# Four attention tiles' exponentials taken set by set with their sums, and two rules of the planner

## The chip, the cores and the metric

The kernel runs on one core of a Trainium2 chip. The metric is the device time of one execution in microseconds, the median of the runs. The engines are called PE (TensorE, matmuls), ACT (ScalarE), DVE (VectorE), POOL (GpSimd) and SP (which issues most DMAs).

## The reference

Windowed attention (4 batches, 8 heads, 768 positions, head size 64), then a gated dense layer and a second dense layer with a rational activation, all in float32:

```python
scores = scale * np.matmul(q_c, k_full.transpose(0, 1, 3, 2))   # 32 queries, 64 keys (8 memory, 56 context)
scores = scores - np.max(scores, axis=-1, keepdims=True)
a = np.exp(scores)
a = a / (np.sum(a, axis=-1, keepdims=True) + 1e-09)
out[:, :, c_start:c_end] = np.matmul(a, v_full)
...
h = (1 / (1 + np.exp(-(x @ w_gate))) * (x @ w_val)) @ w_out     # 3072 x 512 tokens, 1536 features
h = h @ w_in                                                    # 2048 features
g = (a0 + a1*h + a2*h*h + a3*h*h*h) / (1 + abs(b0)*abs(h) + abs(b1)*h*h + 1e-6)
return g @ w_out2
```

## The kernel before

The 3072 tokens are 24 tiles of 128. Attention of a tile yields scores of 128 partitions by eight sets (`NSET`, one for each head) of 64 keys, in two PSUM places (`sp`, one for each half of the heads). Each matrix product of the dense layers is made of three products of rounded halves (`TERMS`), so a weight or an activation is split into a high part (ACT) and a rest (DVE), and weights come as 64-bit words that ACT (`conv_scale`, two activations) and DVE (`conv_bits`) first turn into float32.

Tiles 0 to 3 go first, one by one, in an opening that is written out at lines 1315 to 1384: loads, `attn_qk` (scores), `attn_max` (maximum and subtraction), `attn_exp`, `attn_sum` (sum and reciprocal), `attn_mul`, `attn_t` (four transposes, copied by ACT to `at`) and `pv` (`attn_pv`, product with the values into two places `xp`, split into `x` by ACT and DVE). Between them stand `idle_mm(n)`, n matmuls whose result nobody reads. Scores of a tile at the edge of a sequence (tiles 0 and 5, 6 and 11, ...) are copied to SBUF and masked by POOL; of the others, DVE reads the scores in PSUM. After the opening the loop over (token block, feature) begins with `gate_val` (`h`) for block 0, which needs `x` of tiles 0 to 3, and later tiles' attention is run between dense work: tiles 4 to 7 singly, from tile 8 in pairs, with functions `pair_*`.

The program isn't issued as written. `Recorder` records each call (`call`, line 240) with a duration from a formula (`cost`, line 205) as a task, finds what each depends on (`access`, line 269), and `plan` (line 314) simulates the engines and chooses each engine's order: PE's is the order written; on ACT, DVE, POOL and SP the ready task with the earliest due time (`t.late`) goes next. A due time is worked out backwards from those who need the result. A load of another activation table (exponential, sigmoid, reciprocal root) is charged 1.29 us in the plan. Tiles come from pools with a few places each: `ps` has four PSUM places, taken in turn, so the n-th tile of that pool waits for the users of the one four before it. Every user of a pool's tile other than its first one (`c.first`) depends on the first. What `plan` returns is issued by `emit` at line 471, so all instructions have that line in the profile.

Of the kernel before, what the change touches and what calls it, by code (L numbers as in the profile page):

```python
# [11 lines left out]
F32 = mybir.dt.float32  # L12
# [4 lines left out]
ACTF = mybir.ActivationFunctionType  # L17
ALU = mybir.AluOpType
AX = mybir.AxisListType
PSUM = bass.MemoryType.PSUM  # L20

B, H, S, D = 4, 8, 768, 64
CH, LEFT, RIGHT, NMEM = 32, 16, 8, 8
NT, DM, DFF1, DFF2 = B * S, H * D, 1536, 2048
P = 128
# [6 lines left out]
KEYS = NMEM + LEFT + CH + RIGHT  # L32
OFF1 = WIN - KEYS
NSET = 8
# [140 lines left out]
class Task:  # L175
    def __init__(self, eng):
        self.eng, self.calls, self.deps, self.cells, self.gets = eng, [], set(), set(), []
        self.dur, self.lat, self.bytes, self.start, self.table, self.mark = 0.0, 0.15, 0, None, None, None
        self.window, self.cap, self.soon, self.late, self.fixed = 30.0, None, 0.0, 0.0, False
        self.ordered = True  # L180
# [10 lines left out]
class Recorder:  # L191
# [48 lines left out]
    def call(self, eng, op, args, kw):  # L240
        out = kw.get("out", args[0] if args else None)
        reads = [x for x in (*args[0 if "out" in kw else 1 :], *kw.values()) if isinstance(x, Ref) and x is not out]
        reads = [x for x in reads if x is not kw.get("out")]
        key = {x.cell for x in reads}
        if eng == "tensor" and out.size() > 128:
            key.add(out.cell)
        same = eng == "tensor" and self.open is not None and self.open.key == key
        if same:
            t = self.open
        else:  # L250
            t = Task(eng)
            t.key, t.fixed, t.soon = key, self.fixed, self.ideal
            self.tasks.append(t)
            if eng == "tensor":
                self.open = t
                t.late = t.soon = self.ideal
            if self.noted is not None:
                self.noted.append(t)
        before = t.dur
        self.cost(t, op, args, kw)  # L260
        if eng == "tensor":
            self.ideal += t.dur - before
        t.calls.append((op, args, kw))
        for x, write in [(x, False) for x in reads] + ([(out, True)] if isinstance(out, Ref) else []):
            self.access(t, x, write)
        if eng != "tensor" and self.open in t.deps:
            self.open = None

    def access(self, t, x, write):
        c, box = x.cell, x.box()  # L270
        if c.pool is not None and t not in c.users:
            if c.first is None:
                c.first = t
                t.gets.append(c)
            elif c.first is not t:
                t.deps.add(c.first)
            c.users.add(t)
            t.cells.add(c)
        keep = []
        for b, u, w in c.accesses:  # L280
            if b[0] < box[1] and box[0] < b[1] and b[2] < box[3] and box[2] < b[3]:
                if u is not t and (write or w):
                    t.deps.add(u)
                inside = box[0] <= b[0] and b[1] <= box[1] and box[2] <= b[2] and b[3] <= box[3]
                if write and inside or u is t and w == write and inside:
                    continue
            keep.append((b, u, w))
        keep.append((box, t, write))
        c.accesses = keep
# [24 lines left out]
    def plan(self):  # L314
        tasks = self.tasks
        for t in tasks:
            t.succ = []
        for t in tasks:
            t.missing, t.soft = len(t.deps), []
            for d in t.deps:  # L320
                d.succ.append(t)
            t.ready = 0.0
# [6 lines left out]
        for t in reversed(tasks):  # L329
            t.succ, t.hard = t.succ + t.soft, t.succ  # L330
            if t.eng == "tensor":
                t.late = min([t.soon] + [u.late - t.lat * (u.eng != "tensor") - t.dur for u in t.succ])
                continue
            lat = t.lat + (4.5 if t.bytes else 0)
            cap = t.cap if t.cap is not None else self.DMA_CAP if t.bytes else self.CAP
            t.late = min([t.soon + cap] + [u.late - lat - t.dur for u in t.succ])
        free = dict(self.sizes)
        cells = {c for t in tasks for c in t.cells}
        for c in cells:
# [14 lines left out]
        ready = {e: [t for t in tasks if t.eng == e and not t.missing] for e in engines}  # L354
        busy, dma, table = dict.fromkeys(engines, 0.0), 0.0, None
        order, ends, half, now, stall, left = [], [], None, 0.0, 0.0, len(tasks)
        events = []
        self.stalls = []
        while left:
# [3 lines left out]
            for e in engines:  # L363
# [3 lines left out]
                if e == "tensor":  # L367
                    pick = pe[pe_i : pe_i + 1]
                elif head:
                    pick = head[:1]  # L370
                else:
                    pick = ready[e]
                best = None
                for t in pick:
                    if t.missing or t.ready > now + 1e-9 or best and best.late <= t.late:
                        continue
                    if not t.fixed and e != "tensor":
                        if t.late > now - stall + t.window:
                            continue
                        if t.bytes and dma > now + 7 and t.late > now - stall + 9:  # L380
                            continue
                    need, h = {}, half
                    for c in t.gets:
                        if c.pool == ("t", "half"):
                            if h:
                                h = None
                                continue
                            h = True
                        need[c.pool] = need.get(c.pool, 0) + 1
                    if all(  # L390
                        free[self.real_pool(p)] >= n + 2 * (n == 3) + (0 if t.fixed or p[0] not in (self.ORDERED if t.ordered else "g") else bisect_left(waiting[p], t.key))
                        for p, n in need.items()
                    ):
                        best = t
                if best is None:
                    continue
                t = best
# [10 lines left out]
                if t.table and t.table != table:  # L408
                    table, extra = t.table, 1.29
# [17 lines left out]
                for c in t.cells:  # L427
                    c.left -= 1
                    g = c.group
                    g[2] = max(g[2], end)  # L430
                    if c.left == 0:
                        g[1] += 1
                        if g[1] == 2 or g[1] == g[0] and g is not half:
                            heapq.heappush(ends, (g[2], self.real_pool(c.pool)))
                for u in t.hard:
                    u.missing -= 1
                    u.ready = max(u.ready, end if u.eng != e or e != "tensor" else now + t.dur)
                    if not u.missing and u.eng != "tensor":
                        ready[u.eng].append(u)
                    heapq.heappush(events, u.ready)  # L440
# [4 lines left out]
            if not moved:  # L445
# [5 lines left out]
                for e in engines[1:]:  # L451
                    for t in ready[e]:
                        w = t.late + stall - t.window
# [5 lines left out]
                now = max(nxt, now + 1e-6)  # L459
# [15 lines left out]
def fused_kernel(ctx: ExitStack, tc: tile.TileContext, q, k, v, w1, w2, coef, x2d, w2o, wq2, wqa, wqs, out):  # L475


    nc = Recorder(tc.nc)
# [10 lines left out]
    spool = pool("s", 4)  # L489
# [28 lines left out]
    qs, ks, vs, s_sb, sc_ps, at_sb = {}, {}, {}, {}, {}, {}  # L518
# [22 lines left out]
    def attn_qk(t):  # L541
# [28 lines left out]
        else:  # L570
            sc_ps[t] = sps

    def attn_max(t):
        s = s_sb[t]
        m = spool.tile([P, NSET, 1], F32, tag="m", name=f"m{t}")
        if edge(t):
            nc.vector.tensor_reduce(out=m[:, :, 0], in_=s, axis=AX.X, op=ALU.max)
            nc.vector.tensor_tensor(out=s, in0=s, in1=m.to_broadcast([P, NSET, KEYS]), op=ALU.subtract)
            return
        sv = s.rearrange("p (r h) w -> p r h w", h=2)  # L580
        mv = m.rearrange("p (r h) w -> p r h w", h=2)
        sps = sc_ps.pop(t)
        for h in range(2):
            nc.vector.tensor_reduce(out=mv[:, :, h, 0], in_=sps[h], axis=AX.X, op=ALU.max)
        for h in range(2):
            nc.vector.tensor_tensor(
                out=sv[:, :, h], in0=sps[h], in1=mv[:, :, h].to_broadcast([P, 4, KEYS]), op=ALU.subtract
            )

    def attn_exp(t):  # L590
        s = s_sb[t]
        nc.scalar.activation(out=s, in_=s, func=ACTF.Exp, scale=1.0 / float(D) ** 0.5)

    rs = {}

    def attn_sum(t):
        s = s_sb[t]
        r = rs[t] = spool.tile([P, NSET, 1], F32, tag="r", name=f"r{t}")
        nc.vector.tensor_reduce(out=r[:, :, 0], in_=s, axis=AX.X, op=ALU.add)
        nc.vector.tensor_scalar_add(out=r, in0=r, scalar1=1e-9)  # L600
        nc.vector.reciprocal(out=r, in_=r)

# [1463 lines left out]
```

## Time and profile before

| | |
|---|---|
| median of 3 runs | 1134.45 us (1133.39 to 1134.48) |
| the profiled execution | 1134.46 us |
| its span, first to last instruction | 1132.6 us |
| PE, ACT, DVE busy | 99%, 66%, 77% of the span |
| first `h` matmul starts | 29.86 us |
| activation table loads | 31, of 1.28 us each |

The views used are the busy times of the engines; the same by stretch of time, with the granted clock of TensorE (1.00 is 2.4 GHz, 0.50 is 1.2 GHz); the list of waits; the instructions of one engine in order of time, like ones merged; and the instructions grouped by shape. `out<-in` names the tiles; a tile's name can be that of another one that shares its place.

### The profile page before, as it was taken

What the parts mean: (1) busy time and instruction counts of PE and PEld (TensorE: products, weight loads), DVE (VectorE), ACT (ScalarE), POOL (GpSimd) and SP (SyncE); (2) the same over time, 40 slices, a digit from 0 to 9 for tenths busy, and PEclk for the clock granted to TensorE, in tenths of its full rate; (3) what the DMA queues carried; (4) which work ended last, traced back from release to release, by engine and by line L of the source; (5) the groups of instructions that cost most, each with busy time, mean ns of one, the idle gap of its engine ahead of it and who ended that gap; (6) DMA issues with size and microseconds to landing.
All of it is one profiled execution on the core that took longest, in us unless ns stands there. A gap on an engine that the chain in (4) does not pass through costs nothing.

```text
span 1132.6 us, 20033 instructions
## 1 busy us (share of the span) xinstructions
PE 1120.2 (99%) x7815; PEld 918.5 (81%) x7815; DVE 872.8 (77%) x1184; ACT 750.1 (66%) x1105; POOL 23.1 (2%) x39
## 2 busy tenths in 40 slices
PE   8999999999999999999999999999999999999998
PEld 4787888888888888888888788888888888888887
DVE  5788867774676667565568499999899999789984
ACT  4999556663454466343345599875799974898852
POOL 0000000000000000000000000000000000000000
PEclk8999999999999999999999999999999999999999
DMA  9899699997978799898976576689677788576764
GB/s 371 311 352 360 227 347 363 350 365 259 379 279 324 288 376 387 310 373 291 322 259 246 191 230 220 208 246 342 203 229 225 223 288 307 167 242 219 230 207 143
DMA packets 100318, 318.78 MB, mean 281 GB/s; under 512 B 10752, under 2 KB 11008, under 8 KB 100224
## 3 DMA queue, kind: packets, MB, share of 16 engines
q1 hardware_dynamic: 96192, 303.51, 74.3%
q0 software_dynamic: 3456, 12.58, 6.0%
q8 instruction: 62, 1.02, 0.4%
q10 hardware_dynamic: 576, 1.41, 0.3%
q14 instruction: 32, 0.26, 0.1%
HBM read 240.91 MB, written 63.96 MB: 269 GB/s over the span
## 4 chain that ended last, share of the span: by engine, by line
PE 96%; ACT 1%; DMA 1%; DVE 1%; issue 0%; DVEq 0%
PE acc L471 40%; PE p L471 20%; PE q_X L471 12%; PE h L471 10%; PE q_Z L471 6%; PE q_Y L471 3%; PE xp L471 2%; PE sp L471 1%; PE tp L471 1%; PE idle L471 1%; DMA st<-w_in 0%; DMA k<-k_in 0%; ACT L471 0%; ACT stp L471 0%; DVE s L471 0%
## 5 line engine op out<-in xcount | busy, mean ns | idle before, releaser
L471 PE MATMUL acc<-w2o,G 128*128 128x512 f32 x1152 | 268.4, 389 | 0.0
L471 PEld LDWEIGHTS acc<-w2o,G 128*128 128x128 f32 x1152 | 216.2, 188 | 44.9
L471 PE MATMUL acc<-g,wp 128*128 128x512 f32 x720 | 177.0, 393 | 0.0
L471 PEld LDWEIGHTS acc<-g,wp 128*128 128x128 f32 x720 | 133.3, 188 | 28.3 <-issue 0.2
L471 PE MATMUL q_X<-x,wi 128*128 128x512 f32 x576 | 146.5, 390 | 1.4 <-ACT hb L471 1.4
L471 PE MATMUL h<-x,wp 128*128 128x512 f32 x576 | 138.1, 392 | 1.7 <-ACT sg L471 0.9
L471 PE MATMUL p<-b,wpq_s 128*128 128x512 f32 x576 | 138.4, 389 | 0.0
L471 PEld LDWEIGHTS q_X<-x,wi 128*128 128x128 f32 x576 | 107.9, 188 | 24.7 <-ACT hb L471 2.5
L471 PEld LDWEIGHTS h<-x,wp 128*128 128x128 f32 x576 | 107.2, 188 | 25.0 <-ACT wp L471 1.1
L471 PEld LDWEIGHTS p<-b,wpq_s 128*128 128x128 f32 x576 | 108.1, 188 | 22.5
L471 ACT ACTIVATE st<-st 128x512 f32<-128x512 f32 (+1 forms) x124 | 76.7, 666 | 0.0
L471 PE MATMUL p<-x,wpq_a 128*128 128x512 f32 x288 | 73.2, 389 | 0.0
L471 PE MATMUL q_Z<-x,wi 128*128 128x512 f32 x288 | 73.1, 389 | 0.0
L471 ACT ACTIVATE u<-q,qc 128x1024 f32<-128x1024 f32 x48 | 54.9, 1147 | 14.4 <-DMA q<-u 13.2
L471 PEld LDWEIGHTS p<-x,wpq_a 128*128 128x128 f32 x288 | 54.0, 188 | 11.3
L471 PEld LDWEIGHTS q_Z<-x,wi 128*128 128x128 f32 x288 | 54.1, 188 | 11.2
L471 DVE SCALAR_TENSOR_TENSOR t<-t,cf,u 128x1024 f32<-128x1024 f32 x48 | 61.2, 1278 | 0.0
L471 DVE SCALAR_TENSOR_TENSOR q<-q,u 128x1024 f32<-128x1024 f32 x48 | 58.3, 1219 | 2.2 <-ACT u L471 2.1
L471 ACT ACTIVATE hb<-q_X 128x512 f32<-128x512 f32 x48 | 28.4, 592 | 36.4 <-PE q_X L471 36.3
L471 ACT ACTIVATE u<-u 128x1024 f32<-128x1024 f32 x48 | 50.3, 1055 | 0.4
L471 ACT ACT_TABLE_LOAD x31 | 39.8, 1283 | 15.8 <-PE h L471 7.2
L471 ACT ACTIVATE g<-c 128x512 fp32r<-128x512 f32 x22 | 13.8, 629 | 51.1 <-DVE c L471 51.1
(271 smaller groups left out, 1708.8 us busy)
## 6 DMA issues: line engine op xcount, KB each, us to landing
w2o<-w2o SPq DMA_DIRECT2D x96, 512.0 KB, 4.4
wi<-wq SPq DMA_DIRECT2D x72, 512.0 KB, 4.6
st<-w_in SPq DMA_DIRECT2D x62, 512.0 KB, 7.0
wp<-wqa SPq DMA_DIRECT2D x55, 512.0 KB, 6.6
wpq_s<-wqs SPq DMA_DIRECT2D x48, 512.0 KB, 8.1
wpq_a<-wqa SPq DMA_DIRECT2D x36, 512.0 KB, 7.6
wqa<-wp SPq DMA_DIRECT2D x30, 512.0 KB, 7.5
v<-v_in SPq DMA_DIRECT2D x24, 512.0 KB, 6.4
```

What stands on the lines that cost most here:

```text
L471: getattr(getattr(self.nc, t.eng), op)(*[real(x) for x in args], **{n: real(x) for n, x in kw.items()})
```

## The change

For tiles 0 to 3, `attn_max` no longer subtracts the maximum: it makes `nm`, the negative of the scaled maximum. `attn_exp` then runs one activation for each of the eight sets, of 64 keys, which reads the scores (of tile 0 in SBUF, of tiles 1 to 3 in PSUM), adds `nm` as bias and writes the sum over the keys to `r` (`accum_out`). `attn_sum` only adds 1e-9 and takes the reciprocal. Tiles 4 to 7, which use the same functions, keep the old way. The recorder learns that `accum_out` is written.

In the planner, a tile's users other than the first are tied to the first by `t.after`, not `t.deps`: they may not be issued ahead of it, but the plan no longer makes them wait for its end, and the first one's due time is theirs at the latest, with no latency taken off. And a task that needs an activation table other than the loaded one is passed over while a ready task that needs a table other than that task's is due earlier and ready within 3 us.

```diff
@@ Recorder.call, access
-        reads = [x for x in reads if x is not kw.get("out")]
+        reads = [x for x in reads if x is not kw.get("out") and x is not kw.get("accum_out")]
...
-        for x, write in [(x, False) for x in reads] + ([(out, True)] if isinstance(out, Ref) else []):
+        outs = [x for x in (out, kw.get("accum_out")) if isinstance(x, Ref)]
+        for x, write in [(x, False) for x in reads] + [(x, True) for x in outs]:
...
-                t.deps.add(c.first)
+                t.after.add(c.first)
@@ Recorder.plan
+            t.after -= t.deps
-            t.missing, t.soft = len(t.deps), []
+            t.missing, t.soft = len(t.deps) + len(t.after), []
+            for d in t.after:
+                d.next.append(t)
...
-            t.late = min([t.soon + cap] + [u.late - lat - t.dur for u in t.succ])
+            t.late = min([t.soon + cap] + [u.late for u in t.next] + [u.late - lat - t.dur for u in t.succ])
...
+                        if t.table and t.table != table and any(
+                            u.table and u.table != t.table and u.late < t.late and u.ready < now + 3 for u in pick
+                        ):
+                            continue
...
+                for u in t.next:
+                    u.missing -= 1
+                    u.ready = max(u.ready, now)
+                    if not u.missing and u.eng != "tensor":
+                        ready[u.eng].append(u)
@@ attn_max (the old subtractions now stand under "if t >= 4")
+            sps = sc_ps[t] if t < 4 else sc_ps.pop(t)
...
+        if t < 4:
+            nm = nms[t] = spool.tile([P, NSET, 1], F32, tag="nm", name=f"nm{t}")
+            nc.vector.tensor_scalar(out=nm, in0=m, scalar1=-1.0 / float(D) ** 0.5, scalar2=None, op0=ALU.mult)
@@ attn_exp
+        if t >= 4:
+            nc.scalar.activation(out=s, in_=s, func=ACTF.Exp, scale=1.0 / float(D) ** 0.5)
+            return
+        nm = nms.pop(t)
+        r = rs[t] = spool.tile([P, NSET, 1], F32, tag="r", name=f"r{t}")
+        sps = sc_ps.pop(t, None)
+        for h in range(2):
+            for i in range(4):
+                a = 2 * i + h
+                nc.scalar.activation(
+                    out=s[:, a],
+                    in_=s[:, a] if sps is None else sps[h][:, i],
+                    func=ACTF.Exp,
+                    scale=1.0 / float(D) ** 0.5,
+                    bias=nm[:, a],
+                    accum_out=r[:, a],
+                )
@@ attn_sum (the old sum now stands under "if t >= 4")
```

## Rows read from the trace of the kernel before

**Rows 1.** Page, part 1: busy us, share of the span, instructions of PE.

```profile
PE 1120.2 (99%) x7815; PEld 918.5 (81%) x7815; DVE 872.8 (77%) x1184; ACT 750.1 (66%) x1105; POOL 23.1 (2%) x39
```

**Rows 2.** Stretches: us, then busy us (instructions) by engine, PEclk, DMA share, GB/s.

```profile
10.00:20.00 10.00, 6.20 (x119) 3.82 (x118) 8.59 (x25) 5.31 (x10) 0.00 (x0) 0.88 1.02 406
20.00:30.00 10.00, 10.00 (x255) 7.08 (x251) 6.73 (x14) 7.85 (x18) 0.00 (x0) 0.78 1.03 405
30.00:40.00 10.00, 9.21 (x39) 6.98 (x39) 7.00 (x12) 9.97 (x19) 0.00 (x0) 1.00 0.84 285
200.00:300.00 100.00, 100.00 (x808) 82.91 (x807) 62.51 (x99) 50.57 (x88) 0.00 (x0) 1.00 0.91 337
```

**Rows 3.** Waits of PE over the whole span: us in total, times, longest.

```profile
PE tp L471 <- DVE s L471: 3.1, 2, 1.6
...
PE q_X L471 <- ACT hb L471: 1.4, 2, 0.7
PE h L471 <- ACT sg L471: 0.9, 1, 0.9
PE h L471 <- ACT wp L471: 0.7, 1, 0.7
```

**Rows 4.** PE in order of time, opening: start us, us, work [idle before <-releaser].

```profile
13.50 0.83 PE L471 MATMUL sp<-k,q 64*32 64x64 f32 x61 [0.67 <-issue]
...
18.09 1.09 PE L471 MATMUL tp<-ident,s 128*128 128x128 f32 x4 [1.54 <-DVE s L471]
19.11 1.93 PE L471 MATMUL xp<-at,v 64*64 64x32 f32 x64
...
22.73 1.49 PE L471 MATMUL idle<-ones 128*128 128x512 bf16 x3
...
25.32 0.82 PE L471 MATMUL idle<-ones 128*128 128x512 bf16 x3
...
29.86 7.19 PE L471 MATMUL h<-x,wp 128*128 128x512 f32 x30
```

**Rows 5.** DVE in order of time, opening, columns as in rows 4.

```profile
7.50 0.69 DVE L471 TENSOR_REDUCE m<-s 128x8 f32<-128x512 f32 x1 [6.08 <-POOL s L471]
...
14.35 0.42 DVE L471 TENSOR_REDUCE m<-sp 128x4 f32<-128x256 f32 x1 [1.41 <-PE sp L471]
...
15.09 0.68 DVE L471 TENSOR_TENSOR s<-s,r 128x512 f32<-128x512 f32 x1
```

**Rows 6.** DVE by shape, 0 to 30 us: busy us, mean ns | idle before.

```profile
L471 DVE TENSOR_REDUCE r<-s 128x8 f32<-128x512 f32 x4 | 2.7, 677 | 0.0
L471 DVE TENSOR_TENSOR s<-sp,m 128x256 f32<-128x256 f32 x6 | 2.5, 415 | 0.0
...
L471 DVE TENSOR_SCALAR r<-r 128x8 f32<-128x8 f32 x4 | 0.6, 153 | 0.0
```

**Rows 7.** ACT by shape, whole span, columns as in rows 6.

```profile
L471 ACT ACTIVATE u<-q,qc 128x1024 f32<-128x1024 f32 x48 | 54.9, 1147 | 14.4 <-DMA q<-u 13.2 <-DVE q L471 1.1
L471 ACT ACTIVATE u<-u 128x1024 f32<-128x1024 f32 x48 | 50.3, 1055 | 0.4
...
L471 ACT ACTIVATE at<-tp 128x512 f32<-128x512 f32 x16 | 9.0, 592 | 1.2 <-PE tp L471 1.2
...
L471 ACT ACTIVATE s<-s 128x512 f32<-128x512 f32 x7 | 4.4, 631 | 4.5 <-DVE s L471 4.5
...
L471 ACT ACTIVATE sc<-sc 128x1 f32<-128x1 f32 x2 | 0.4, 203 | 0.2 <-DVE sc L471 0.2
```

**Rows 8.** ACT in order of time, columns as in rows 4.

```profile
39.22 1.14 ACT L471 ACTIVATE wp<-wfgv 128x512 fp32r<-128x512 f32 x2
...
90.93 1.28 ACT L471 ACT_TABLE_LOAD   x1
...
95.21 0.60 ACT L471 ACTIVATE sg<-h 128x512 f32<-128x512 f32 x1
```

**Rows 9.** PE in order of time near 113 us.

```profile
113.62 0.60 PE L471 MATMUL tp<-ident,s 128*128 128x128 f32 x4
```

More of the change, by code (lines that the diff above doesn't have):

```diff
@@ L177, in __init__ @@
         self.eng, self.calls, self.deps, self.cells, self.gets = eng, [], set(), set(), []
+        self.after = set()
         self.dur, self.lat, self.bytes, self.start, self.table, self.mark = 0.0, 0.15, 0, None, None, None
@@ L316, in plan @@
         for t in tasks:
-            t.succ = []
+            t.succ, t.next = [], []
         for t in tasks:
-            t.missing, t.soft = len(t.deps), []
+            t.after -= t.deps
+            t.missing, t.soft = len(t.deps) + len(t.after), []
+            for d in t.after:
+                d.next.append(t)
             for d in t.deps:
@@ L331, in plan @@
             if t.eng == "tensor":
-                t.late = min([t.soon] + [u.late - t.lat * (u.eng != "tensor") - t.dur for u in t.succ])
+                t.late = min([t.soon] + [u.late for u in t.next] + [u.late - t.lat * (u.eng != "tensor") - t.dur for u in t.succ])
                 continue
@@ L571, in attn_qk @@
             sc_ps[t] = sps
+    nms = {}
     def attn_max(t):
@@ L577, in attn_max @@
             nc.vector.tensor_reduce(out=m[:, :, 0], in_=s, axis=AX.X, op=ALU.max)
[L578 to L588, printed above, removed]
+            if t >= 4:
+                nc.vector.tensor_tensor(out=s, in0=s, in1=m.to_broadcast([P, NSET, KEYS]), op=ALU.subtract)
+        else:
+            sv = s.rearrange("p (r h) w -> p r h w", h=2)
+            mv = m.rearrange("p (r h) w -> p r h w", h=2)
+            sps = sc_ps[t] if t < 4 else sc_ps.pop(t)
+            for h in range(2):
+                nc.vector.tensor_reduce(out=mv[:, :, h, 0], in_=sps[h], axis=AX.X, op=ALU.max)
+            if t >= 4:
+                for h in range(2):
+                    nc.vector.tensor_tensor(
+                        out=sv[:, :, h], in0=sps[h], in1=mv[:, :, h].to_broadcast([P, 4, KEYS]), op=ALU.subtract
+                    )
@@ L590, in attn_exp @@
+        if t < 4:
+            nm = nms[t] = spool.tile([P, NSET, 1], F32, tag="nm", name=f"nm{t}")
+            nc.vector.tensor_scalar(out=nm, in0=m, scalar1=-1.0 / float(D) ** 0.5, scalar2=None, op0=ALU.mult)
+    rs = {}
     def attn_exp(t):
         s = s_sb[t]
-        nc.scalar.activation(out=s, in_=s, func=ACTF.Exp, scale=1.0 / float(D) ** 0.5)
-    rs = {}
+        if t >= 4:
+            nc.scalar.activation(out=s, in_=s, func=ACTF.Exp, scale=1.0 / float(D) ** 0.5)
[3 more added lines that the diff above has]
+        sps = sc_ps.pop(t, None)
+        for h in range(2):
+            for i in range(4):
[7 more added lines that the diff above has]
+                    accum_out=r[:, a],
+                )
@@ L596, in attn_sum @@
     def attn_sum(t):
         s = s_sb[t]
-        r = rs[t] = spool.tile([P, NSET, 1], F32, tag="r", name=f"r{t}")
-        nc.vector.tensor_reduce(out=r[:, :, 0], in_=s, axis=AX.X, op=ALU.add)
+        if t >= 4:
+            r = rs[t] = spool.tile([P, NSET, 1], F32, tag="r", name=f"r{t}")
+            nc.vector.tensor_reduce(out=r[:, :, 0], in_=s, axis=AX.X, op=ALU.add)
+        r = rs[t]
         nc.vector.tensor_scalar_add(out=r, in0=r, scalar1=1e-9)
```

## The prediction, made before the changed kernel was run

> **What bounds the kernel now.** I read the busy shares first, then the stretches, then what TensorE (PE) waits for, then the start in order of time. PE is busy for 1120.2 of 1132.6 us [rows 1]. From 200 to 300 us it is busy in all of it, at the full clock [rows 2]; the reader should see that there every other engine only has to be in time, so nothing that ScalarE (ACT) or VectorE (DVE) saves there shortens the run. PE's waits with an engine's name are few: 3.1 us for the attention tiles `s` in the opening, then 0.7 us for a weight split (`wp`), 0.9 us for a sigmoid (`sg`) and 1.4 us for copies of `hb` [rows 3]. The last three sum to 3.0 us; that is all that the work after the opening can give back. The opening itself ends at 29.86 us, when the first `h` matmul of the dense layers starts [rows 4]. Before it PE runs attention of four tiles and fillers, and whatever moves 29.86 moves the end by as much, so long as weights keep up.
>
> The profiled execution took 1134.46 us, 1.86 more than its span; the median of the three runs is 1134.45, so no correction lies between them. About 0.2% (2.3 us) is what a measurement of this kernel can tell from no change.
>
> **What sets 29.86 us.** PE's order is written out and the diff leaves it alone. The scores of tile 3 end at 13.50 + 0.83 = 14.33; then PE waits for tile 0's `s`, transposes it, waits for tile 1's, transposes that at 18.09, and starts the first value product (`xp`, tile 0) at 19.11 [rows 4]; the two waits are the 3.1 us named above. From there to the first `h` it stands in no wait: 10.75 us of transposes, products and fillers. So the start of that first `xp` is the number to forecast. Why tile 0's `s` is late is in DVE's order: its maximum starts at 7.50, but its scaling by the reciprocal only at 15.09, since DVE stands 1.41 us at the maximum of tile 3 ahead of it [rows 5].
>
> The clock counts too: the granted clock is 0.88 over 10 to 20 us and 0.78 over 20 to 30 [rows 2], after the two waits. Three fillers take 1.49 us at 22.73 but 0.82 at 25.32 [rows 4]: the 1.2 GHz level against 2.4. If 0.78 is a mixture of the two levels, 4.4 of the ten microseconds from 20 to 30 are at the lower one, and with the last microsecond before 20 about 5.3 of the work behind 19.11; at the full clock it would take some 2.6 us less.
>
> **Off DVE.** For each of tiles 0 to 3 the subtraction of the maximum goes (two of 0.415 us, or one of the whole width) and the sum over keys (0.677); a product of 128x8 comes, like the `TENSOR_SCALAR` of 0.153 [rows 6]. About 1.2 us a tile, 4.9 in all. DVE then has no queue ahead of tile 0's scaling, and PE's two waits for `s` are no longer DVE's doing.
>
> **Onto ACT.** Each tile's one exponential of 128x512 (0.631 us) becomes eight of 128x64 with a bias from memory and a sum written out. The trace has none, so I build the price. From 512 to 1024 columns an activation grows from 0.631 to 1.055, so 0.83 ns a column and 0.203 fixed, which is also what a 128x1 activation takes [rows 7]. A bias from memory costs 1.147 - 1.055 = 0.092 [rows 7]. Two activations of a row take 1.14 us where one takes 0.62, so neighbours overlap by 0.10 [rows 8]. Hence 0.203 + 0.053 + 0.092 - 0.10 = 0.25 us each, without the sum. For writing the sum no row exists: at least nothing, at most a further whole 128x1 activation (0.20). I take 0.10, that activation less the overlap, as its nearest row is a short instruction in a stream: 0.35 us. Tiles 1 to 3 read PSUM, for which I take off 0.04 (the copies `at<-tp` from PSUM take 0.592 [rows 7]): 0.31. So 2.8 us for tile 0 and 2.5 for each other, against 0.53 each in a stream: 8.1 us more on ACT (4.9 and 11.3 at the bounds). What covers it is ACT's idle time: it is busy 5.31 of the first of those ten-microsecond stretches and 7.85 of the second, but 9.97 of 10 from 30 to 40 [rows 2]. 6.8 us of idle time stand against 8.1, so some of the scaling of weights slides behind 30 us. There it has room only because ACT also prepares weights that are not due next.
>
> **The new chain to the first `xp`.** The scores of tiles 1 to 3 stay in PSUM until their eighth exponential has ended, where the subtraction freed them before. There are four PSUM places: scores of tile 3 take those of tile 1, the transposes those of tile 2, and the first `xp` those of tile 3. Maximum 0 ends at 7.50 + 0.69, the product at 8.35. Tile 0's exponentials end at 11.15, tile 1's at 13.65, tile 2's at 16.15; then the copy of the first transpose (0.5), and tile 3's from 16.65 to 19.15. The first `xp` starts at 19.15 against 19.11: the wait for DVE has become a wait for ACT of the same length, **nought** on the sum. At 0.25 and 0.21 the sets end at 10.35, 12.05 and 13.75; tile 3's must wait for its scores and maximum (15.35) and end at 17.05: 2.0 us earlier. At 0.45 and 0.41 tile 1's end at 15.25, so the scores of tile 3 start there, not at 12.6, and tile 3's set ends at 22.35: 3.2 us later. Both ends stay in the range. Queued behind these exponentials on ACT are the copies of transposes, the splits of `x` and the scaling of the first weights; PE waits for all of them.
>
> **Places as order.** Users of a tile other than its first no longer wait, in the plan, for the first's end and latency; only their order stays. That takes no instruction away and adds none. Without it each of seven exponentials would be planned behind the first one's end. But due times of all first users change, so orders on ACT, DVE and SP can change anywhere. I put it at nothing, as PE has cover nearly everywhere [rows 2]; if that cover went at one place, the loss would be like the present waits, 0.7 to 0.9 us each.
>
> **The table rule.** A table load takes 1.28 us [rows 8]. At 90.93 ACT loads the table for an exponential, then loads the other back, and the sigmoid starts at 95.21, for which PE waited 0.9 us [rows 3, 8]. The rule holds such an exponential back while a sigmoid due sooner is at most 3 us from ready, so the sigmoid goes first and the wait goes: 0.9 us off. The exponential then comes some 5 us later; what hides that is that the next transposes of an `s` stand at 113.62 on PE [rows 9], nearly 20 us on. Were that cover gone, PE would wait for the tile as it now waits for the sigmoid.
>
> **Sum.** 1134.46 + 0 - 0.9 = 1133.6 us, no change that can be told.
>
> **The rivals.** *Cheap sums.* If the sum is written at no cost, the first `xp` comes 2.0 us earlier: 1134.46 - 2.0 - 0.9 = 1131.6. If PE's gaps then become so short that the clock doesn't fall, 2.6 more: 1128.9. For it: the fall came after two waits that DVE's order made. Against it: PE would still stand between the transposes and the first `xp`. The Trainium skill, page "TensorE: Matmul & The Clock Gate", Part 1, says that idleness gates the clock and activity releases it; the trace agrees as far as the lower clock comes behind the waits.
>
> *ACT becomes the bound* (the slower side). With a sum as dear as a whole short activation, the chain is 3.2 us late: 1134.46 + 3.2 = 1137.7, and 1139 if the 11.3 us also make PE wait for the split of the second feature's weights, where it already stands 0.7 us [rows 3]. It decides above about 0.41 us for an exponential that reads PSUM, or lower if scalings of weights are planned between the sets: each is two activations of 0.5 us or a little more in a stream. For it: the plan prices an exponential at 0.19 to 0.23 us (line 227), so its order is made for an ACT that is faster than the one on the chip. The Trainium skill, page "ScalarE: Activation LUTs", Rules for kernel authors, gives adding and multiplying to VectorE rather than ScalarE; this change goes against that, and the rows bear it out where the exponential costs more than about 0.31.
>
> *The plan is remade elsewhere.* Three new waits of 0.7 to 0.9 us would give about 1136.7 without the gain at 95 us; losing the `hb` waits (1.4) and the weight wait (0.7) would give 1131.5.
>
> *The change doesn't do what it says*: if the rule at 95 us never bites, 1134.5.
>
> **Chances.** No change, 1132.3 to 1136.6, holds 0.44 (the forecast and the rule that never bites). Cheap sums 0.22, ACT as the bound 0.18, a remade plan 0.16, of it 0.06 faster and 0.10 slower. Faster 0.28, slower 0.28. The range goes from 1129 (cheap sums and a full clock) to 1139 (dear sums with a late split); beyond these lie less than 2 in 10.
>
> **What would show it.** Right: eight short `s` activations for each of four tiles at 0.25 to 0.45 us from start to start, no `TENSOR_REDUCE r<-s` on DVE in the opening, the first `xp` within 1 us of 19.11 and right behind tile 3's last exponential, the granted clock again half for some microseconds, no PE wait for `sg` near 95 us, PE without gaps from 200 to 600. Wrong: the first `h` more than 2.3 us from 29.86; ACT idle before the first `xp` (then something else gates it); new PE waits after 40 us that sum to over 2 us.

## The result, and the profile after

| | before | after |
|---|---|---|
| median | 1134.05 us (4 runs, 1133.39 to 1134.48) | 1144.27 us (4 runs, 1143.67 to 1144.86) |
| ratio | | 1.0089, 95% interval 1.0074 to 1.0104 |
| span of the profiled execution | 1132.6 us | 1142.0 us |
| first `h` matmul starts | 29.86 us | 29.25 us |

The change made the kernel 10.2 us slower, where 1133.6 (1129 to 1139) was predicted. The opening went almost as forecast in time, and the loss came later, in a place that the prediction had called safe.

The stretches first (columns as in rows 2), of the kernel after:

```profile
10.00:20.00 10.00, 5.41 (x136) 3.39 (x134) 5.66 (x18) 10.00 (x61) 0.00 (x0) 1.00 1.03 406
20.00:30.00 10.00, 10.00 (x245) 6.97 (x238) 5.23 (x11) 7.74 (x18) 0.00 (x0) 0.83 1.03 405
...
850.00:1070.00 220.00, 220.00 (x957) 179.31 (x956) 200.68 (x217) 177.44 (x222) 8.88 (x11) 1.00 0.74 235
```

Beside [rows 2]: from 10 to 20 us ACT is now full (10.00 of 10, it was 5.31), and PE's lower clock takes less of the opening (0.83 in the second row alone, where before it was 0.88 and 0.78). The last row is the one to stop at. PE is busy in all 220 us at the full clock, yet it gets fewer matmuls done than the kernel before in the same stretch:

```profile
850.00:1070.00 220.00, 220.00 (x973) 182.15 (x972) 203.54 (x221) 179.59 (x226) 9.53 (x11) 1.00 0.74 238
```

973 there, 957 here: 1.6% less work in a stretch without a gap. What PE waits for in the kernel after (us in total, times, longest; it answers to [rows 3]) can't account for it; the two largest stand in the opening:

```profile
PE xp L485 <- ACT at L485: 2.1, 1, 2.1
PE tp L485 <- DVE s L485: 1.8, 1, 1.8
...
PE q_X L485 <- ACT hb L485: 1.4, 2, 0.7
...
```

Of the waits in [rows 3], `sg` and `wp` are gone, `hb` is as it was, and the 3.1 us for `s` in the opening became 1.8 for `s` and 2.1 for `at`. Yet the page's first part gives PE 1130.2 us of busy time where it was 1120.2 [rows 1], for the same 7815 instructions. So the instructions themselves became longer. Grouped by shape (busy us, mean ns | idle before), 262 to 1077 us, after and then before:

```profile
L485 PE MATMUL acc<-w2o,G 128*128 128x512 f32 x888 | 209.1, 390 | 0.0
L485 PE MATMUL q_X<-x,wi 128*128 128x512 f32 x576 | 149.9, 395 | 1.4 <-ACT hb L485 1.4
L485 PE MATMUL p<-b,wpq_s 128*128 128x512 f32 x552 | 135.9, 394 | 0.0
L485 PE MATMUL q_Y<-x,wi 128*128 128x512 f32 x144 | 37.5, 395 | 0.0
```

```profile
L471 PE MATMUL acc<-w2o,G 128*128 128x512 f32 x924 | 216.7, 389 | 0.0
L471 PE MATMUL q_X<-x,wi 128*128 128x512 f32 x576 | 146.5, 390 | 1.4 <-ACT hb L471 1.4
L471 PE MATMUL p<-b,wpq_s 128*128 128x512 f32 x558 | 134.1, 389 | 0.0
L471 PE MATMUL q_Y<-x,wi 128*128 128x512 f32 x144 | 36.5, 389 | 0.0
```

`q_X`, `q_Y` and `p` take 5 to 6 ns more each, `acc` 1 at most. (The means overlap their neighbours, as matmuls are pipelined. From the start of one `q_Z` or `q_Y` to the next it is 226.67 ns on average before and 233.33 after.) What the slower groups have in common is pool `b`: their streamed operand (the one that passes through PE, while the weights stand in it) lies there, 1728 matmuls of 512 columns in all. And what the change did to pool `b` is plain once one looks for it: `nm` is a new tile of 8 floats in pool `s`, with four places, 128 bytes a partition, and pool `s` is laid out ahead of pool `b`. In the kernel before, pool `b` begins at byte 163104 of a partition, in the kernel after at 163232. The pools `w`, `x` and `g` stay. Modulo 256 all four begin at 32 before; after, `b` begins at 160, so that the 1728 matmuls have their two operands 128 bytes apart and the other 2880 have them at 0 as before.

The time between landmarks on PE, from the starts in the traces (us):

| | first `h` | `h` to first `p` | `p` to first `q` | `q` to PE's last |
|---|---|---|---|---|
| before | 29.86 | 226.1 | 370.2 | 502.7 |
| after | 29.25 | 223.8 | 375.6 | 509.7 |

Up to the first `p` at 253 us the change had gained some 3 us; from there on it lost 12.4, in the last two columns (5.4 and 7.0), where the matmuls on pool `b` stand.

### The profile page after: what moved, and what is told of

Its sections match the earlier page's. It is cut to its first block, busy times and chain, and to the rows that moved or that the text cites. A ratio compares the mean times of both kernels' runs of the same rounds, so it can differ in the third digit from the quotient of the medians.

```text
span 1142.0 us, 20079 instructions
## 1 busy us (share of the span) xinstructions
PE 1130.2 (99%) x7815; PEld 917.7 (80%) x7815; DVE 870.0 (76%) x1177; ACT 758.5 (66%) x1163; POOL 23.1 (2%) x39
## 4 chain that ended last, share of the span: by engine, by line
PE 98%; ACT 1%; DMA 0%; DVE 0%; issue 0%; POOL 0%; ACTq 0%
PE acc L485 41%; PE p L485 20%; PE q_X L485 12%; PE h L485 12%; PE q_Z L485 6%; PE q_Y L485 3%; PE xp L485 2%; PE sp L485 1%; PE tp L485 1%; ACT s L485 1%; DMA k<-k_in 0%; PE idle L485 0%; DVE m L485 0%; ACT hb L485 0%; ACT at L485 0%
## 5 line engine op out<-in xcount | busy, mean ns | idle before, releaser
L485 PE MATMUL q_X<-x,wi 128*128 128x512 f32 x576 | 149.9, 395 | 1.4 <-ACT hb L485 1.4
L485 PE MATMUL p<-b,wpq_s 128*128 128x512 f32 x576 | 141.8, 394 | 0.0
L485 PEld LDWEIGHTS p<-x,wpq_a 128*128 128x128 f32 x288 | 54.1, 188 | 12.1
L485 DVE TENSOR_TENSOR c<-u,p 128x512 f32<-128x512 f32 x41 | 28.2, 687 | 24.3 <-PE p L485 23.9
```

What stands on the lines that cost most here:

```text
L485: getattr(getattr(self.nc, t.eng), op)(*[real(x) for x in args], **{n: real(x) for n, x in kw.items()})
```

## The experiments

**1. Only the place of `nm` is put back.** The kernel after, with `nm` in a pool of its own, opened behind pool `b`; the order of work on every engine is that of the kernel after.

```diff
+    npool = pool("n", 4)
...
-            nm = nms[t] = spool.tile([P, NSET, 1], F32, tag="nm", name=f"nm{t}")
+            nm = nms[t] = npool.tile([P, NSET, 1], F32, tag="nm", name=f"nm{t}")
```

> The changed kernel with its only new tile, nm (4 places of 32 bytes), in a pool of its own behind all others, so that every other tile lies where it lay before; the order on every engine is that of the changed kernel. Both theories of place: matmuls that read pool b go from 233.3 to 226.7 ns from start to start, the 12.3 us between 262 and 1077 us go, and 1144.3 becomes about 1132.0 us (2 us under before). Theory 'order': 1144.3 us, no change.

Measured: 1132.93 us (10 runs, 1132.21 to 1133.43), ratio to before 0.9984 (0.9975 to 0.9993). The first part of its page, and its late stretch:

```profile
PE 1119.0 (99%) x7815; PEld 919.1 (81%) x7815; DVE 868.8 (77%) x1177; ACT 755.6 (67%) x1163; POOL 23.1 (2%) x39
```

```profile
850.00:1070.00 220.00, 220.00 (x972) 182.21 (x972) 204.04 (x222) 177.87 (x223) 9.54 (x11) 1.00 0.75 237
```

Back to 972 matmuls, and 11.3 us faster than the change as it was made. `q_X` is at 146.5 us again. This is also the version that beats both kernels, by 1.4 us over before.

**2. Only the place is moved.** The kernel before with 128 idle bytes ahead of pool `b`, which POOL fills once; nothing else.

```diff
+    pad = pool("pad", 1).tile([P, 32], F32, name="pad")
+    tc.nc.gpsimd.memset(pad.ap(), 0.0)
     bpool = pool("b", 8)
```

> The kernel before with an unused tile of 128 bytes ahead of pool b and nothing else: the order on PE, ACT, DVE and SP is that of before, the b tiles start 128 bytes further on. Both theories of place: the same 12.3 us are lost, 1134.05 becomes about 1146.3 us. Theory 'order': 1134.05 us, no change.

Measured: 1147.19 us (4 runs), ratio 1.0106 (1.0091 to 1.0121). The loss is there without the exponentials and without either rule of the planner, so 128 bytes are enough to cause it. From 850 to 1070 us it does 957 matmuls, as the kernel after does:

```profile
850.00:1070.00 220.00, 220.00 (x957) 179.37 (x956) 200.31 (x216) 177.40 (x220) 9.54 (x11) 1.00 0.73 231
```

**3. Absolute or relative place.** The kernel before with the 128 bytes ahead of everything, so that all pools move alike.

```diff
     const = pool("const", 1)
...
+    pad = const.tile([P, 32], F32, name="pad")
+    tc.nc.gpsimd.memset(pad.ap(), 0.0)
```

> The kernel before with an unused tile of 128 bytes ahead of all others, so that every tile of every pool, weights and moving operands alike, starts 128 bytes further on. Theory 'absolute place': all of some 4,500 matmuls of 512 columns take 6.7 ns more, 1134 becomes about 1164 us. Theory 'relative place': no change, 1134 us. Theory 'order': no change.

Measured: 1134.71 us (10 runs), ratio 1.0002 (0.9992 to 1.0011). Pool `b` has the same absolute remainder as in the kernel after, and nothing is lost: what counts is where it lies relative to something else.

**4. The other way about.** The 128 bytes behind the weights' pool `w` and ahead of `x`, so that in every matmul of 512 columns one operand moves against the other. In `acc<-w2o,G` it is the weights (`G`, pool `g`) that move, and the streamed `w2o` stays in pool `w`; in all other groups the weights stay.

```diff
     wpool = pool("w", 20)
+    pad = pool("pad", 1).tile([P, 32], F32, name="pad")
+    tc.nc.gpsimd.memset(pad.ap(), 0.0)
     xpool = pool("x", 4)
```

> The kernel before with 128 bytes left free behind the weights' pool, so that the weights keep their place and every moving operand (pools x, g, t, s and b) lies 128 bytes further, modulo 256, from them than before; the order of work is untouched. The theory of the relative place: not only the matmuls on pool b but all matmuls of 512 columns, some 4,600 of them, take 233.3 ns instead of 226.7, so 4,600 x 6.6 ns = 30 us more, about 1164 us (1158 to 1168); h and acc rise as well as p and q, and the stretch from the first h to the first p grows by some 3 % (226.1 to about 232 us). Rival, that only the place of pool b counts (its absolute place, or something its tiles share): 1147 us, as with the 128 bytes ahead of b alone. Rival, that what counts is the distance of the pools x and g from b: no loss, 1134 us.

Measured: 1160.70 us (4 runs), ratio 1.0228 (1.0210 to 1.0246). By shape, whole span:

```profile
L471 PE MATMUL acc<-w2o,G 128*128 128x512 f32 x1152 | 275.9, 395 | 0.0
L471 PE MATMUL q_X<-x,wi 128*128 128x512 f32 x576 | 150.0, 395 | 1.4 <-ACT hb L471 1.4
L471 PE MATMUL h<-x,wp 128*128 128x512 f32 x576 | 140.8, 397 | 1.0 <-ACT wp L471 0.6 <-ACT sg L471 0.4
```

Now `acc` and `h` are slow too, which never touch pool `b`: it is the distance between a matmul's weights and its streamed operand. The 30 us expected were too many: `q_Z` is at the 233.2 ns forecast, but `h` at 232.3 against 227.6 before, and 25.9 us over 4608 matmuls are 5.6 ns each.

**5. Two more distances in the kernel.** The kernel after with 128 further bytes ahead of `b` (256 in all), and the kernel before with 64 (16 floats in the pad).

```diff
+    pad = pool("pad", 1).tile([P, 32], F32, name="pad")
+    tc.nc.gpsimd.memset(pad.ap(), 0.0)
     bpool = pool("b", 8)
```

> The changed kernel as it is, nm in its old place, with 128 unused bytes more ahead of pool b, so that b starts 256 bytes further on than before. Theory 'distance to the weights modulo 256 bytes': matmuls that read b are back at 226.7 ns and 1144.3 becomes about 1132.9 us, as in e1. Rival 'any shift away from the old place costs': about 1144 us or more.

> The kernel before with 64 bytes left free ahead of pool b instead of 128; the order of work is untouched. If the streams of matmuls with constant operands carry over, a distance of 64 bytes costs 228.9 - 226.7 = 2.2 ns a matmul and not 6.7, over some 2,000 matmuls 4.5 us: 1138 to 1140 us. If any distance other than 0 modulo 256 costs the same 12.3 us in the kernel, 1147 us; if only 128 does, 1134 us.

Measured: with 256 bytes 1133.12 us (10 runs), ratio 0.9987 (0.9978 to 0.9997), so a shift of 256 bytes costs nothing, and neither does the place of `nm` there. With 64 bytes 1144.66 us (4 runs), ratio 1.0088 (1.0072 to 1.0104): twice the 4.5 us expected. The groups that run among themselves fit what was expected (`q_Z`, `q_Y` and `p<-b,wpq_a` at 228.9 ns from start to start), but `p<-b,wpq_s` is at 230.0 and `q_X` at 230.5, and even `acc<-w2o,G`, whose own distance is unchanged, went from 226.7 to 228.6. A matmul among others of another distance pays for its neighbours; a stream of constant operands doesn't show that. The trace of the kernel after shows it too: in the groups of `acc<-w2o,G` that stand right behind a group of `q`, the first three matmuls take 231.6, 232.5 and 230.8 ns from start to start, the fourth 226.6; before, all take 226.5 to 226.9.

**6. The distance by itself.** Streams of 24 matmuls 128x512 (fp32r, the 32-bit type of the dense layers' operands) with one weight tile and one streamed tile at chosen places; no other engine works beside them, and the rest of the computation is left out. It ran once.

```python
for i in range(24):
    nc.tensor.matmul(pt, lhsT=w[:, w0 : w0 + P], rhs=x[:, x0 : x0 + 512], start=i == 0, stop=i == 23)
```

> This kernel leaves out the whole computation of the reference: it only runs streams of 24 matmuls of 128x512 on loaded data, 36 streams with the moving operand at 0, 32, 64 ... 1120 bytes from a multiple of 2048 and the weights at 0, then ten streams each with the weights at 32 and at 128 bytes; its output is no result. Theory 'absolute place' (a matmul is slower when its moving operand starts at certain bytes): from start to start about 227 ns for most starts and about 233 ns for some, the same for all three places of the weights, so start 160 slow and start 32 fast with the weights at 32. Theory 'relative place' (what counts is the distance to the weights): with the weights at 128 bytes the slow starts move by 128. Theory 'order' (the changed order of ScalarE, VectorE and the DMA queue slows TensorE): all streams at the same 227 ns, as nothing else runs.

PE in order of time (columns as in rows 4); the step from one start to the next, over 24, is the time of a matmul. `zaa` to `zai` have the weights at 0 and the streamed operand at 0, 32, 64, ... 256 bytes; `zbk` and `zbl` have the weights at 32 bytes and the streamed operand at 0 and 32:

```profile
20.24 5.60 PE L34 MATMUL zaa<-x,w 128*128 128x512 f32 x24
25.68 5.77 PE L34 MATMUL zab<-x,w 128*128 128x512 f32 x24
31.28 5.67 PE L34 MATMUL zac<-x,w 128*128 128x512 f32 x24
36.79 5.77 PE L34 MATMUL zad<-x,w 128*128 128x512 f32 x24
...
64.82 5.63 PE L34 MATMUL zai<-x,w 128*128 128x512 f32 x24
70.28 5.77 PE L34 MATMUL zaj<-x,w 128*128 128x512 f32 x24
...
220.80 5.76 PE L34 MATMUL zbk<-x,w 128*128 128x512 f32 x24
226.40 5.61 PE L34 MATMUL zbl<-x,w 128*128 128x512 f32 x24
231.84 5.77 PE L34 MATMUL zbm<-x,w 128*128 128x512 f32 x24
```

5.44 us or 226.7 ns at distance 0; 5.60 or 233.3 at 32; 5.51 or 229.5 at 64; again 5.60 with the weights at 32 and the other operand at 0, and 5.44 with both at 32. Distances of 96 to 224 lie at 233 to 234 (232 to 234 with the weights at 128 bytes), 256 at 5.46 or 227.5, and the row repeats up to 1120 bytes.

**7. Own weights or the next ones, and other widths.** The same kind of streams, with places taken in turn; the rest of the computation is left out. It ran once.

```diff
+        w0, x0 = ws[i % len(ws)], xs[i % len(xs)]
```

> Leaves out the whole computation: it is a row of streams of 24 matmuls each, one constant weight tile and one moving tile with places chosen by hand (bytes, modulo 256, of the distance from the weights to the moving operand). First stream at distance 0, second at 128, as in the earlier streams: 226.7 and 233.3 ns from start to start. Then two weight places, 0 and 128, taken in turn, with the moving operand at 0 and 128 in turn (each matmul at distance 0 from its own weights and 128 from the next one's), and the other way round (128 from its own, 0 from the next one's). Theory A (a matmul's reads collide with the reads of its own weights' place): the first of the two is at about 226.7 ns and the second at 233.3. Theory B (they collide with the load of the next matmul's weights, which runs beside it on PEld): the first at 233.3 and the second at 226.7. If both are slow or both are half slow, neither. Two weight places with the moving operand at 0: the mean lies half way, about 230 ns, by either. Then 256 and 384 columns at distance 0, 64 and 128: if the collision is with the load of 128 columns, the loss a matmul is the same 6.7 ns (113 to 120 ns at 256 columns); if it is in proportion to the columns read, it is 3.3 ns at 256 and 5.0 at 384. Last, the same distances from 0 to 256 with 16-bit operands of 512 columns: no theory here says whether these show the loss; with half the bytes read, half of the loss or none is the likelier.

`zab` is at distance 0, `zac` at 128. `zad` takes two weight places in turn, at distance 0 from its own and 128 from the next one's; `zae` is the reverse. `zas` has 16-bit operands at a distance of 128 bytes:

```profile
20.74 5.60 PE L47 MATMUL zab<-x,w 128*128 128x512 f32 x24
26.18 5.75 PE L47 MATMUL zac<-x,w 128*128 128x512 f32 x24
31.77 5.64 PE L47 MATMUL zad<-x,w 128*128 128x512 f32 x24
37.25 5.68 PE L47 MATMUL zae<-x,w 128*128 128x512 f32 x24
42.77 5.74 PE L47 MATMUL zaf<-x,w 128*128 128x512 f32 x24
48.35 5.68 PE L47 MATMUL zag<-x,w 128*128 128x512 f32 x24
...
101.20 5.34 PE L47 MATMUL zas<-xb,wb 128*128 128x512 bf16 x23
106.38 5.34 PE L47 MATMUL zat<-xb,wb 128*128 128x512 bf16 x24
```

226.7 and 233 ns as before, but 228.4 for `zad` and 230.0 for `zae`: both lie between, so neither theory holds alone; the time depends on the next weights as well as on a matmul's own. That taking places in turn costs by itself is ruled out by the kernel before, whose matmuls change weights all the time, always at distance 0, and take 226.7. The two shares don't simply add: `zaf`, two weight places with the streamed operand at 0, is at 232.5, where either theory had 230. At 256 columns distance 0 has no advantage (119.7 ns at 0, 118.0 at 64, 118.5 at 128); at 384 it is 173.5, 173.1 and 175.5. So the loss is neither a fixed amount for each load of weights nor in proportion to the columns. 16-bit streams show no loss at any distance: 5.18 us for `zas`, 215.8 ns each. How the chip comes by these numbers stays open.

The Trainium skill, page "TensorE: Matmul & The Clock Gate", Part 2, "Step-by-step: what each phase is for", says that weights and streamed operand have read ports of their own, and "Loading the next tile's weights doesn't steal SBUF read bandwidth from the running matmul", with 215.7 ns for a matmul of 512 columns. The 16-bit streams agree with both (215.8 ns, whatever the distance). The fp32r matmuls of this kernel don't: they take 226.7 ns at best, 3% more where the two operands lie badly to each other, and 228.4 where only the next weights do. That it is read bandwidth which they lose is not shown; that they lose time is, and here the measurement decides.

**8. The table rule undone.** Experiment 1 without the rule on activation tables.

```diff
-                        if t.table and t.table != table and any(
-                            u.table and u.table != t.table and u.late < t.late and u.ready < now + 3 for u in pick
-                        ):
-                            continue
```

> As e1_nm_last (changed kernel, nm behind all other tiles), without the rule on activation tables. Theory 'rule': TensorE's wait for the sigmoid near 95 us (0.9 us) is back, 1132.9 becomes about 1133.8 us; the opening up to 40 us is as in e1. Rival 'due times': the sigmoid's wait went because due times changed, so no wait near 95 us and 1132.9 us.

Measured: 1136.90 us (10 runs, 1134.28 to 1137.40), ratio 1.0016 (1.0007 to 1.0025), 4.0 us over experiment 1. Without the rule, ACT in order of time, then PE:

```profile
92.57 1.28 ACT L481 ACT_TABLE_LOAD   x1
93.87 0.63 ACT L481 ACTIVATE sg<-sg 128x512 f32<-128x512 f32 x1
94.52 1.28 ACT L481 ACT_TABLE_LOAD   x1
95.81 0.60 ACT L481 ACTIVATE c<-h 128x512 f32<-128x512 f32 x1
```

```profile
93.58 0.66 PE L481 MATMUL tp<-ident,wfo 128*128 128x128 f32 x4
96.46 4.61 PE L481 MATMUL h<-x,wp 128*128 128x512 f32 x12 [2.23 <-ACT c L481]
```

and with it, ACT in the kernel after:

```profile
92.31 0.58 ACT L485 ACTIVATE c<-h 128x512 f32<-128x512 f32 x1
...
95.02 1.28 ACT L485 ACT_TABLE_LOAD   x1
96.32 0.63 ACT L485 ACTIVATE sg<-sg 128x512 f32<-128x512 f32 x1
```

(The tile names are those of places: `sg<-sg` is an attention tile's exponential, `c<-h` the sigmoid.) Without the rule PE stands 2.2 us, and then the granted clock is 0.68 from 95 to 100 us and 0.98 from 100 to 105, some 3.4 us at half clock, or 1.7 lost. Together 3.9. (Two of the ten runs lie at 1134.3 and 1134.4, the others from 1135.9 to 1137.4; why is not settled.) From the first `h` to the first `p` it takes 227.8 us, 4.0 more than in experiment 1.

**9. The planner's rules alone.** The kernel before with both rules and the old exponentials: the change without its parts in `attn_max`, `attn_exp` and `attn_sum`.

```diff
-                t.deps.add(c.first)
+                t.after.add(c.first)
...
+                        if t.table and t.table != table and any(
```

> The kernel before with both rules of the planner and the old exponentials, so with no nm and every pool where it lay. Theory 'exponentials': the first h matmul and the wait for the weight split near 37 us (0.7 us) are as before, only the sigmoid's wait of 0.9 us goes: 1134.3 becomes about 1133.4 us. Rival 'planner': the weight split comes in time because the order changed, and the time is e1's 1132.9 us or less, so that the exponentials set by set bring nothing.

Measured: 1136.68 us (10 runs, 1133.73 to 1139.74), ratio 1.0021 (1.0006 to 1.0035). The runs fall into two groups, five from 1133.7 to 1135.3 us and five from 1138.1 to 1139.7; what parts them is not settled, and the traced one (1135.28) is of the faster group. In it the first `xp` stands at 19.08 us, but DVE is now waited for three times (3.7 us, two before that `xp` and one behind it) and the first `h` comes at 32.03, 2.2 us later than before. The third wait is 0.6 of this; 0.8 stands within the matmuls of a later `xp`, with no releaser in the trace; and the lower clock lies wholly behind the first `xp` (6.8 us, where it was 5.3), which costs 0.75 more. Neither theory came: there is no wait for `wp`, but PE still waits 0.5 us for `sg`. So it is with the set-by-set exponentials that the planner's rules pay in the opening. Without the table rule (8) or without the exponentials (9) the median is some 0.2% over before; with all of it, and the place mended, 0.16% under it.

**10. One tile fewer.** Experiment 1 with tile 3 the old way, to see what the chain of exponentials costs; the loads of tile 0 are kept first in the queue (`nc.fixed`), as they are in experiment 1.

```diff
-            if t >= 4:
+            if t >= 3:
...
+        nc.fixed = True
         load_qk(0)
+        nc.fixed = False
```

> As e1_nm_last, with tile 3's exponentials in the old way (subtraction and sum on VectorE, one activation), so three tiles set by set; tile 0's loads are held first in the queue, as they are in e1. Theory 'ScalarE holds the first xp': 8 x 0.29 us of ScalarE become about 0.55, the wait of 1.5 us for the copy `at` shrinks, the first xp starts some 1.5 us earlier than in e1 (19.34) and 1132.9 becomes about 1131.4 us. Rival 'PE or weights hold the first h': the first xp comes earlier, but the first h or a later one waits instead: 1132.9 us.

Measured: 1139.98 us (4 runs), ratio 1.0046 (1.0030 to 1.0063), 7 us over what either theory gave at the most. PE in the opening:

```profile
17.89 1.06 PE L485 MATMUL xp<-at,v 64*64 64x32 f32 x57 [0.39 <-ACT at L485]
...
23.86 1.09 PE L485 MATMUL tp<-ident,s 128*128 128x128 f32 x4 [2.62 <-DVE s L485]
...
36.30 0.96 PE L485 MATMUL h<-x,wp 128*128 128x512 f32 x1
```

The first `xp` does come 1.45 us earlier than in experiment 1 (19.34), as it no longer stands behind tile 3's exponentials. But then PE waits 2.6 us for tile 3 from DVE, the granted clock is 0.50 from 20 to 30 us and 0.64 from 30 to 40, and the first `h` starts 6.9 us later. An earlier first `xp` isn't an earlier `h`.

## Why the prediction was wrong, by its own steps

**What bounds the kernel now: the step that failed.** "There every other engine only has to be in time" is true of the waits, and from it the prediction took the length of every matmul as given. The sum then had two terms, the opening and the wait at 95 us, and left out a third: the time of the matmuls themselves. `nm` entered only as "a product of 128x8 … like the `TENSOR_SCALAR` of 0.153". Its product takes 0.16 to 0.17 us of DVE a tile, and its 128 bytes cost 11.3 us of PE (experiment 1; 12.9 in experiment 2). By the traces the missing term is 1728 matmuls on pool `b` that take 6.2 ns longer from start to start, 10.6 us, and 1.5 us on their neighbours whose own places stayed: 12.1 of the 12.4 lost behind the first `p`. Nothing in the trace of before shows this price; that the groups of 512 columns took nearly the same there (389 to 393 ns) was the sign that all pools lay alike, and it could be read either way.

**"PE without gaps from 200 to 600"** was named as a sign that the forecast is right. It came true while 5.4 us were lost between the first `p` and the first `q`. Gaps and waits can't show longer instructions; a count of matmuls in a full stretch, or mean durations, can.

**The price of an exponential: right.** ACT in the opening, tile 1's sets from PSUM and then tile 0's from SBUF:

```profile
9.51 0.31 ACT L485 ACTIVATE s<-sp,nm 128x64 f32<-128x64 f32 x1
9.71 0.20 ACT L485 ACTIVATION_READ_ACCUMULATOR s<-sp,nm 128x1 f32 x1
9.80 0.31 ACT L485 ACTIVATE s<-sp,nm 128x64 f32<-128x64 f32 x1
...
12.20 0.38 ACT L485 ACTIVATE s<-s,nm 128x64 f32<-128x64 f32 x1
12.44 0.23 ACT L485 ACTIVATION_READ_ACCUMULATOR s<-s,nm 128x1 f32 x1
12.53 0.37 ACT L485 ACTIVATE s<-s,nm 128x64 f32<-128x64 f32 x1
```

From start to start 0.29 and 0.33 us, where 0.31 and 0.35 were taken; the sum is an instruction of its own and costs 0.09 (9.71 to 9.80), where 0.10 was taken. The 32 exponentials take ACT from 8.68 to 18.49 us, 7.7 us more than the old four, where 8.1 were taken, and DVE is busy for 5.0 us less in the first 30 us (18.2, now 13.2), where 4.9 were taken. So "cheap sums" didn't come, and "ACT becomes the bound" not with its 3.2 us: ACT does hold the first `xp`, but at the time that was forecast.

**The first `xp`: right in size, not in its way.** It starts at 19.25 us (19.15 forecast, 19.11 before). PE in order of time:

```profile
16.12 1.07 PE L485 MATMUL tp<-ident,s 128*128 128x128 f32 x8 [1.83 <-DVE s L485]
19.25 1.14 PE L485 MATMUL xp<-at,v 64*64 64x32 f32 x64 [2.06 <-ACT at L485]
...
29.25 1.97 PE L485 MATMUL h<-x,wp 128*128 128x512 f32 x7
```

The wait for ACT was forecast, though the copy `at` was to come ahead of tile 3's sets and came behind all of them. That DVE would have "no queue ahead of tile 0's scaling" was wrong: ACT took tile 1's sets before most of tile 0's, and DVE again stood at the maximum of tile 3, 1.46 us until 14.31, ahead of tile 0's scaling at 15.28. Tile 0's last exponential ended only at 13.98 on ACT; with DVE's maxima of tile 3 (14.31 and 14.72) between the steps that follow, this makes the 1.8 us that PE still waits for `s`. That the start came out within 0.1 us is therefore in part luck.

**The clock in the opening: right that it falls; for how long is chance.** The 5.3 us at the lower level behind the first `xp` were read from 0.88 and 0.78 [rows 2]; the two make 6.8 us in all, 1.5 of it ahead of 19.11. After the change 0.83 makes 3.4 us. 1.9 us less at half the clock are worth 0.95; the stretch from the first `xp` to the first `h` went from 10.75 to 10.0. But this is not shown to be the change's doing. In experiment 1 and in the one with 256 bytes, which have the same order of work, the lower level takes 6.8 us of the opening (0.81 and 0.85; 0.92 and 0.74), and the first `h` starts at 29.45 and 30.29. With the order of before it starts at 29.86, and at 30.13 to 30.64 in experiments 2, 3 and 4 and with 64 bytes (5). So the 0.6 us gained up to the first `h` is no more than these starts scatter.

**The table rule: the mechanism right, the size not.** The `sg` wait went, and the exponential's table load moved from 90.93 [rows 8] to 95.02 without harm, as forecast. But 0.9 us is what the wait cost in the old plan. Beside the new exponentials it would have been 2.2 us and a fall of the clock: the rule is worth 4.0 us (experiment 8). An edit's price depends on the other edits.

**Places as order: not nothing.** It was put at nothing. The `wp` wait of 0.7 us near 37 us went, which only a rival counted. It went with the old exponentials too (experiment 9), but there the first `h` starts 2.2 us later, so that it was the order is likely and not shown. With `sg` this makes 1.6 of the 2.3 us gained from `h` to `p`; the other 0.7 is not settled. Alone, without the new exponentials, the two rules put the first `h` at 32.03 us, 1.4 us behind the latest of those with the order of before.

**The sum without the missing term.** With `nm` behind `b` the kernel takes 1132.93 us, 0.7 under the 1133.6 predicted. The `sg` term held; that the rest came so near is in part luck, since the `wp` wait and another 0.7 us between `h` and `p` were gained that the sum doesn't hold. What the prediction never looked at decided.

## What to carry to other kernels

A new tile, however small, moves every pool laid out behind it: look up the places of the operands of the bounding engine before and after, and put small new tiles last. On this chip an fp32r matmul of 512 columns was fastest, of the distances tried (steps of 32 bytes), where its weights and its streamed operand have the same place modulo 256 bytes (226.7 ns against 229 to 234). And where the bounding engine has no gaps, compare its count of instructions in one full stretch, or their mean durations: a slower engine looks as busy as a fast one.

## What the runs showed of the hardware that was not expected

- A matmul of 128x512 in fp32r takes 226.7 to 227.7 ns from start to start at a distance of 0 modulo 256 bytes between weights and streamed operand, 229.5 at 64, and 232 to 234 at the other distances tried; in the kernel that is up to 2.3% (experiment 4). In 16-bit it takes 215.8 at all distances tried. The reason is open.
- A matmul also pays for its neighbours' distance: 226.7 to 228.6 ns for `acc<-w2o,G` when only pool `b` moved by 64 bytes, and 230.8 to 232.5 for the first three behind a group of `q` when it moved by 128.
- Writing an activation's sum appears as an instruction of its own, `ACTIVATION_READ_ACCUMULATOR`, which adds 0.09 us in a stream.
